# One-column products of a decode-attention backward pass, streamed 48 columns wide with a stride-0 operand

## The chip, the cores and the metric

One core of a Trainium2 chip. The metric is device time of one launch in microseconds (us). The kernel before takes 462.21 us (median of 3 runs, 458.82 to 466.44). A run can fall in a slow state (e1's profiled run took 472.17 us, its other three 458.97 to 465.29); all comparisons below use fast runs. A ratio is the mean time of one kernel's fast runs over that of the other's from the same rounds, so it isn't quite the ratio of the medians quoted beside it.

## The reference, cut to what matters

A gated mix of two branches, forward and backward in one launch. The branch that costs the time is attention of a single query over a cache: 32 heads, 4,096 keys of 128 values each, bf16.

```python
scores = einsum("bhqd,bhkd->bhqk", q, k_cache) * Dh ** -0.5   # one query per head
p = softmax(scores)
o = einsum("bhqk,bhkd->bhqd", p, v_cache)
out = g * (o @ wo) + (1 - g) * mlp(x)
# and the gradients of everything, among them dK and dV of all 32 heads
```

K and V are read (2.1 MB per head) and dK and dV written (2.1 MB per head); with the weights 165 MB cross the memory interface. Since there is one query, S = K q, dP = V dO, o = V'p and dq = K'ds are all matrix times vector.

## The kernel before

For S and dP the contraction runs over the head dimension, and the kernel transposes K and V for them. A head's K tile is `[128, 32, 128]` bf16; the kernel views two neighbouring bf16 as one fp32 and transposes 128x128 fp32 blocks on TensorE, 16 for K and 16 for V. ScalarE copies each four of them out of the PSUM tile that they were written to (256 copies of 587 ns on average). Then each product loads 128x128 weights and streams one or two columns; the page counts 5,916 weight loads to 5,916 matmuls.

```python
def transposes(src, c):                       # line L550: fp32 transposes; L552: the copy out
    ...
    nc.tensor.transpose(tp[:, t, :], flat[:, k * P:(k + 1) * P], ident_f[:])
    ...
    nc.scalar.copy(sb[...], tp[...])

def products(out, tb, c, vec):                # L559: S and dP, 2 columns each, 64 per head
    for t in range(4):
        k = c * 4 + t
        for par in range(2):
            nc.tensor.matmul(out[:, 2 * k:2 * k + 2], lhsT=tb[:, t, par, :], rhs=vec[:, par, :],
                             start=(par == 0), stop=(par == 1))

# in period(h), one head:
S, Z, O, MM = A[:, 0:J], A[:, 32:64], A[:, 64:65], A[:, 128:256]        # one PSUM tile
DP, DQ, PT = B[:, 0:J], B[:, 64:65], B[:, 128:256]                      # another
for j in range(J):                            # L618: o, 1 column, 32 per head
    nc.tensor.matmul(O, lhsT=vts[h][:, j, :], rhs=st["e"][:, j:j + 1], ...)
for j in range(J):                            # L670: dq, 1 column, 32 per head
    nc.tensor.matmul(DQ, lhsT=kts[h][:, j, :], rhs=ds[:, j, 0:1], ...)
```

VectorE multiplies the outer products dK and dV (L574). Loads are issued by SyncE in program order. K and V come three heads ahead, when the K buffer of the head before is released by its last dq product (SyncE waited 302.2 us for these products, in 27 waits); every fourth head the weights for a later group are loaded, behind that head's K and V:

```python
for h in range(H):
    hh, g = h % G, h // G                     # groups of G = 4 heads
    load_k(h + 3)
    load_v(h + 3)
    if hh == 0 and g + 1 < NG:
        prep_steps(g + 1, h)                  # q of the next group: needs wq; dO: needs wo
    if hh == 3:
        load_wo(g + 2)
        if g % 2 == 0:
            load_wq(g // 2 + 1)
    period(h)
```

Of the kernel before, what the change touches and what calls it, by code (L numbers as in the profile page):

```python
# [8 lines left out]
ALU = mybir.AluOpType  # L9
# [7 lines left out]
def kernel(  # L17
# [24 lines left out]
    nc = tc.nc  # L42
    P = 128
# [3 lines left out]
    J = Sk // P  # L47
    RC = D // P
    G = 4
    NG = H // G  # L50
    GD = G * Dh
    WG = 8
# [14 lines left out]
    dwq_v = out_4.rearrange("(rc r) c -> r rc c", r=P)  # L67
    wo_v = A_wo.rearrange("(g p i) n -> g p i n", p=P, i=G)
    dwo_v = out_5.rearrange("(g p i) n -> g p i n", p=P, i=G)
    w1_v = B_w1.rearrange("(rc r) f -> r rc f", r=P)  # L70
# [40 lines left out]
    kts, vts, wqs, wos = {}, {}, {}, {}  # L111
# [16 lines left out]
    def load_wo(g):  # L128
        if g < NG:
            wos[g] = wts.tile([P, G, D], BF16, name="wo_g", tag="wo_g", bufs=3)  # L130
            nc.sync.dma_start(wos[g][:], wo_v[g])
# [3 lines left out]
    def load_w2(c):  # L135
# [23 lines left out]
        out=ident_f[:], in_=ident_f[:], compare_op=ALU.not_equal, fill=1.0,  # L159
# [5 lines left out]
    nc.vector.tensor_copy(ident_bf[:], ident_f[:])  # L165
    mask4 = const.tile([P, 1, G], BF16, name="mask4")
    red4 = const.tile([P, P // G], BF16, name="red4")
# [62 lines left out]
    for i in range(3):  # L230
        t = const.tile([P, 2, G, 2, 2], BF16, name=f"qd2_{i}")
# [7 lines left out]
    def add(name, kind, fn, deps=(), head=0):  # L239
        steps.append((name, kind, fn, tuple(deps), head))  # L240
# [3 lines left out]
    def slot(h, p=2, d=1):  # L244

        slot_no[0] += 1
        room = {"P": p, "D": d, "T": 99}
        for kind in ("T", "D", "P"):
            for st in list(steps):
                name, k, fn, deps, head = st  # L250
                if k != kind or head > h or not room[k]:
                    continue
                if all(done.get(x, 1 << 30) < slot_no[0] for x in deps):
                    fn()
                    done[name] = slot_no[0]
                    steps.remove(st)
                    room[k] -= 1
# [70 lines left out]
    o_all = const.tile([P, H], BF16, name="o_all")  # L328
    dq_all = const.tile([P, H], BF16, name="dq_all")
# [213 lines left out]
    sts = {}  # L543

    def transposes(src, c):
        tp = tr_ps.tile([P, 4, P], F32, name="tr", tag="tr")
        flat = f32v(src[:].rearrange("p j d -> p (j d)"))
# [3 lines that stand above are left out]
        sb = tsb.tile([P, 4, P], F32, name="tT", tag="tT")  # L551
        nc.scalar.copy(sb[:].rearrange("p a b -> p (a b)"), tp[:].rearrange("p a b -> p (a b)"))  # L552
        return sb[:].rearrange("p a b -> p (a b)").bitcast(BF16).rearrange("p (a b two) -> p a two b", a=4, two=2)

    def products(out, tb, c, vec):
        for t in range(4):
            k = c * 4 + t
            for par in range(2):
                nc.tensor.matmul(out[:, 2 * k:2 * k + 2], lhsT=tb[:, t, par, :], rhs=vec[:, par, :],  # L559
                                 start=(par == 0), stop=(par == 1))  # L560

    def k_chunk(h, c, ts):
        ts.append(transposes(kts[h], c))

    def s_chunk(h, c, ts):
        gp = gps[h // G]
        if c == 0:
            sts[h] = {"A": sa_ps.tile([P, 512], F32, name="sA", tag="sA")}
        products(sts[h]["A"][:, 0:J], ts[c], c, gp["x2"][:, 0, h % G])

    def outer(dst, col, row, half):
        n = J // 2
# [7 lines left out]
    def dk_half(h, half):  # L580
        if h < 0:
            return
        st = sts[h]
        if half == 0:
            st["dK"] = outs.tile([P, J, Dh], BF16, name="dK_sb", tag="dVK")
        outer(st["dK"], st["ds"], gps[h // G]["qd"][:, 0, (h % G) * Dh:(h % G + 1) * Dh], half)
        if h == H - 1:
            a, b = half * (J // 2), (half + 1) * (J // 2)
            nc.gpsimd.dma_start(dKv[h][:, a:b, :], st["dK"][:, a:b, :])
        elif half == 1:  # L590
            nc.gpsimd.dma_start(dKv[h], st["dK"][:])  # L591
        if half == 1:
            sts.pop(h)
# [9 lines left out]
    def period(h):  # L603
        gp = gps[h // G]
        st = sts[h]
        nxt = h + 1 < H
        A = st["A"]
        S, Z, O, MM = A[:, 0:J], A[:, 32:64], A[:, 64:65], A[:, 128:256]
        B = st["B"] = sb_ps.tile([P, 512], F32, name="sB", tag="sB")
        DP, DQ, PT = B[:, 0:J], B[:, 64:65], B[:, 128:256]  # L610
        vec = gp["x2"][:, 1, h % G]
        tv, tk = [], []
        V = lambda c: tv.append(transposes(vts[h], c))
        dP = lambda c: products(DP, tv[c], c, vec)

        def o_part(a, b):
            for j in range(a, b):
                nc.tensor.matmul(O, lhsT=vts[h][:, j, :], rhs=st["e"][:, j:j + 1], start=(j == 0), stop=(j == J - 1))  # L618

        m32 = small.tile([P, 1], F32, name="m32", tag="m32")  # L620
        nc.vector.reduce_max(m32[:], S, axis=AX.X)  # L621
        V(0)
        dk_half(h - 1, 0)
        V(1)
        nc.tensor.transpose(MM, m32[:].to_broadcast([P, P]), ident_f[:])  # L625
        negM = small.tile([P, 1], F32, name="negM", tag="negM")
        nc.vector.tensor_reduce(negM[:], MM, axis=AX.X, op=ALU.max, negate=True)  # L627
        dk_half(h - 1, 1)
        e = st["e"] = small.tile([P, J], BF16, name="e_bf", tag="e_bf")
        V(2)  # L630
        dP(0)
        nc.scalar.activation(e[:], S, ACT.Exp, bias=negM[:], scale=1.0)
        V(3)
        dP(1)
        nc.tensor.matmul(Z, lhsT=ones_bf[:], rhs=e[:], start=True, stop=True)  # L635
        zs = small.tile([P, 1], F32, name="zs", tag="zs")
        nc.vector.reduce_sum(zs[:], Z, axis=AX.X)  # L637
        rz = st["rz"] = small.tile([P, 1], F32, name="rz", tag="rz")
        nc.vector.reciprocal(rz[:], zs[:])
        p_bf = st["p"] = small.tile([P, J, 2], BF16, name="p_bf", tag="p_bf")  # L640
        nc.scalar.activation(p_bf[:], e[:].unsqueeze(2).to_broadcast([P, J, 2]), ACT.Copy, scale=rz[:])
        dP(2)
        o_part(0, J)
        dP(3)
        slot(h)
        part = small.tile([P, 1], F32, name="part", tag="part")
        pj = small.tile([P, J], F32, name="pj", tag="pj", bufs=1)
        nc.vector.scalar_tensor_tensor(pj[:], in0=DP, scalar=1.0, in1=e[:], op0=ALU.mult, op1=ALU.mult,  # L648
                                       accum_out=part[:])
        dv_half(h, 0)  # L650
        nc.tensor.transpose(PT, part[:].to_broadcast([P, P]), ident_f[:])  # L651
        if nxt:
            k_chunk(h + 1, 0, tk)
            k_chunk(h + 1, 1, tk)
        dd = small.tile([P, 1], F32, name="dd", tag="dd")
        dj = small.tile([P, P], F32, name="dj", tag="dj", bufs=1)
        nc.vector.tensor_scalar(dj[:], PT, rz[:], None, ALU.mult, ALU.add, accum_out=dd[:])
        ds = st["ds"] = small.tile([P, J, 2], BF16, name="ds_bf", tag="ds_bf")
        nc.vector.scalar_tensor_tensor(ds[:], in0=DP.unsqueeze(2).to_broadcast([P, J, 2]), scalar=dd[:], in1=p_bf[:],  # L659
                                       op0=ALU.subtract, op1=ALU.mult)  # L660
        dv_half(h, 1)
        nc.vector.tensor_scalar(o_all[:, h:h + 1], O, rz[:], None, ALU.mult)
        if nxt:
            s_chunk(h + 1, 0, tk)
            k_chunk(h + 1, 2, tk)
        slot(h)
        if nxt:
            s_chunk(h + 1, 1, tk)
        for j in range(J):
            nc.tensor.matmul(DQ, lhsT=kts[h][:, j, :], rhs=ds[:, j, 0:1], start=(j == 0), stop=(j == J - 1))  # L670
        if nxt:
            k_chunk(h + 1, 3, tk)
            s_chunk(h + 1, 2, tk)
        nc.scalar.copy(dq_all[:, h:h + 1], DQ)  # L674
        if nxt:
            s_chunk(h + 1, 3, tk)
        kts.pop(h)
        vts.pop(h)
        slot(h)


    dwqt = {}
    CL = (NG - 1) * GD

# [19 lines left out]
    for h in range(H):  # L704
        hh, g = h % G, h // G
# [3 lines that stand above are left out]
            rest = steps[:]  # L709
# [10 lines left out]
        if h == H - 3:  # L720
            for rc in range(RC):
                add(f"dwq{rc}", "D", dwq_make(rc), (f"dqb{NG - 2}",), h + (rc + 1) // 2)
                add(f"dwqs{rc}", "T", lambda rc=rc: dwq_store(rc), (f"dwq{rc}",), h)
# [79 lines left out]
```

## Time and profile before

| | before |
|---|---|
| time | 462.21 us, profile 462.1 us |
| TensorE busy / mean granted clock | 84% / 0.61 |
| VectorE busy | 67% |
| DMA | 164.93 MB, 357 GB/s on average |
| fp32 transposes (L550) | 1,024 |
| one- and two-column products of S, dP, o and dq | 4,096 |

"Granted clock" is the share of full speed that the page gives for TensorE. In the row PEclk of the page each digit is one of 40 slices of the span, in tenths; 5 is half speed. The nines at its start are no full clock: the record of the clock begins near 20 us, and transposes at 15.35 us ran at the half-clock pace (eight in 1.78 us). The row DMA shows in tenths how busy the 16 DMA engines were. The lines themselves stand in the prediction.

### The profile page before, as it was taken

How to read it: one execution, taken by the hardware profiler on the slowest of the kernel's cores; microseconds unless marked ns; L12 is line 12 of the kernel's file. 1: busy time of each engine (PE TensorE's matmuls, PEld its weight loads, DVE VectorE, ACT ScalarE, POOL GpSimd, SP SyncE). 2: the span in 40 equal slices, each digit the busy share in tenths (PEclk: the TensorE clock that was granted, in tenths of full speed). 3: DMA queues.
4: the chain of work that ended last, by engine and by line, in shares of the span. 5: the costliest groups of instructions: out<-in, count | busy, mean ns of one | idle time of the engine just before them, and what ended most of it. 6: DMA issues, size and time to landing. Idle time of an engine off the chain costs nothing.

```text
span 462.1 us, 13671 instructions
## 1 busy us (share of the span) xinstructions
PE 389.3 (84%) x5916; PEld 363.1 (79%) x5916; DVE 311.1 (67%) x785; ACT 186.3 (40%) x410; POOL 49.3 (11%) x95
## 2 busy tenths in 40 slices
PE   2799999999999999799988999799898999999600
PEld 1688989899888888788877888788887888888500
DVE  4275443745578877787758876767768977777892
ACT  2444333443434444354443444345543544444200
POOL 0000000000000100010000110002100100011321
PEclk9965555656556665687565656656656756556555
DMA  7999999958798899999999899997999999845995
GB/s 268 416 382 372 424 419 418 359 242 319 309 374 313 321 386 381 419 399 331 419 422 364 308 399 393 409 411 280 374 396 357 380 395 377 338 179 218 400 405 200
DMA packets 26328, 164.93 MB, mean 357 GB/s; under 512 B 2812, under 2 KB 2812, under 8 KB 10012
## 3 DMA queue, kind: packets, MB, share of 16 engines
q1 hardware_dynamic: 14156, 82.03, 46.1%
q0 software_dynamic: 12112, 82.03, 44.3%
q8 instruction: 46, 0.75, 0.6%
q14 instruction: 14, 0.11, 0.1%
HBM read 82.03 MB, written 82.03 MB: 355 GB/s over the span
## 4 chain that ended last, share of the span: by engine, by line
PE 61%; DMA 18%; DVE 9%; ACT 7%; issue 2%; SPq 0%; ACTq 0%; DVEq 0%
PE tr L550 35%; DMA wo_g<-in_A_wo_dram 10%; DMA wq_g<-in_A_wq_dram 8%; ACT tT L552 5%; PE sB L670 5%; PE sA L559 5%; PE h_ps L404 3%; PE sA L618 3%; PE sB L559 2%; DVE junk L375 2%; DVE junk L278 2%; PE sB L651 2%; PE sA L625 1%; DVE zs L637 1%; PE ap_ps L356 1%
## 5 line engine op out<-in xcount | busy, mean ns | idle before, releaser
L552 ACT COPY tT<-tr 128x512 f32<-128x512 f32 x256 | 148.9, 587 | 206.2 <-PE tr L550 205.2
L550 PE MATMUL tr<-ident_f,Kn 128*128 128x128 f32 x512 | 121.8, 400 | 0.0
L550 PE MATMUL tr<-ident_f,Vn 128*128 128x128 f32 x512 | 119.9, 396 | 0.0
L559 PEld LDWEIGHTS <-tT 128*128 128x128 bf16 x2048 | 90.1, 107 | 36.6 <-ACT tT L552 29.5
L550 PEld LDWEIGHTS tr<-ident_f,Vn 128*128 128x128 f32 x512 | 93.3, 209 | 0.0
L550 PEld LDWEIGHTS tr<-ident_f,Kn 128*128 128x128 f32 x512 | 91.7, 207 | 0.3 <-issue 0.3
L574 DVE TENSOR_TENSOR dV_sb<-p_bf,qd 128x2048 bf16<-128x2048 bf16 x64 | 77.9, 1218 | 0.0
L574 DVE TENSOR_TENSOR dK_sb<-ds_bf,qd 128x2048 bf16<-128x2048 bf16 x64 | 77.7, 1216 | 0.0
L559 PE MATMUL sA<-qd,tT 128*128 128x2 bf16 x1024 | 48.4, 168 | 19.0 <-ACT dq_all L674 12.8
L559 PE MATMUL sB<-qd,tT 128*128 128x2 bf16 x1024 | 44.0, 166 | 0.0
L621 DVE TENSOR_REDUCE m<-sA 128x1 f32<-128x32 f32 x32 | 6.1, 192 | 51.9 <-PE sA L559 42.4
L601 POOL DMA_DIRECT2D out_dram<-dV_sb x32 | 17.6, 551 | 184.5 <-DVE dV_sb L574 127.8
L591 POOL DMA_DIRECT2D out_dram<-dK_sb x31 | 16.6, 535 | 190.8 <-DVE dK_sb L574 170.9
L618 PEld LDWEIGHTS <-Vn 128*128 128x128 bf16 x1024 | 31.2, 100 | 5.0 <-issue 5.0
L618 PE MATMUL sA<-e_bf,Vn 128*128 128x1 bf16 x1024 | 30.8, 164 | 3.0
L670 PE MATMUL sB<-ds_bf,Kn 128*128 128x1 bf16 x1024 | 31.6, 165 | 1.7 <-DVE ds_bf L659 1.2
L278 DVE SCALAR_TENSOR_TENSOR junk<-wo_g,da_bc 128x640 bf16<-128x640 bf16 x32 | 26.3, 822 | 8.6 <-DMA wo_g<-in_A_wo_dram 8.0
L670 PEld LDWEIGHTS <-Kn 128*128 128x128 bf16 x1024 | 29.7, 103 | 2.0 <-issue 2.0
L627 DVE TENSOR_REDUCE negM<-sA 128x1 f32<-128x128 f32 x32 | 9.3, 291 | 25.6 <-PE sA L625 25.6
L375 DVE SCALAR_TENSOR_TENSOR junk<-wq_g,dq_bc 128x1024 bf16<-128x1024 bf16 x20 | 24.3, 1216 | 0.1
L637 DVE TENSOR_REDUCE zs<-sA 128x1 f32<-128x32 f32 x32 | 6.1, 192 | 21.9 <-PE sA L635 21.6
L651 PE MATMUL sB<-ident_f,part 128*128 128x128 f32 x32 | 13.2, 413 | 8.7 <-DVE pj L648 8.5
(144 smaller groups left out, 313.9 us busy)
## 6 DMA issues: line engine op xcount, KB each, us to landing
Kn<-in_A_k_cache_dram SPq DMA_DIRECT2D x32, 1024.0 KB, 7.8
Vn<-in_A_v_cache_dram SPq DMA_DIRECT2D x32, 1024.0 KB, 13.9
out_dram<-dV_sb POOLq DMA_DIRECT2D x32, 1024.0 KB, 6.5
out_dram<-dK_sb POOLq DMA_DIRECT2D x31, 1024.0 KB, 8.7
wq_g<-in_A_wq_dram SPq DMA_DIRECT2D x4, 1280.0 KB, 6.4
wo_g<-in_A_wo_dram SPq DMA_DIRECT2D x8, 640.0 KB, 14.3
out_dram<-wo_g POOLq DMA_DIRECT2D x8, 640.0 KB, 9.7
out_dram<-dwq_t POOLq DMA_DIRECT2D x5, 896.0 KB, 8.8
```

The lines of the kernel that those rows point to most:

```text
L278: nc.vector.scalar_tensor_tensor(junk[:, 0:D], in0=wos[g][:, i, :], scalar=1.0, in1=da_bc[:], op0=ALU.mult, op1=ALU.mult, accum_out=gp["do ...
L375: nc.vector.scalar_tensor_tensor(junk[:], in0=wqs[w][:, rc, :], scalar=1.0, in1=dq_bc[:, w * WG * Dh:(w + 1) * WG * Dh], op0=ALU.mult, op1 ...
L404: nc.tensor.matmul(hps["t"][:, fc:fc + 1], lhsT=w1_sb[:, rc, :].rearrange("p (q c) -> p q c", c=FCN)[:, :, fc], rhs=x_bf[:, rc:rc + 1], st ...
L550: nc.tensor.transpose(tp[:, t, :], flat[:, k * P:(k + 1) * P], ident_f[:])
L552: nc.scalar.copy(sb[:].rearrange("p a b -> p (a b)"), tp[:].rearrange("p a b -> p (a b)"))
L559: nc.tensor.matmul(out[:, 2 * k:2 * k + 2], lhsT=tb[:, t, par, :], rhs=vec[:, par, :], start=(par == 0), stop=(par == 1))
L574: nc.vector.tensor_tensor(dst[:, a:b, :].rearrange("p j (a b) -> p j a b", b=2), col[:, a:b, :].unsqueeze(2).to_broadcast([P, n, Dh // 2, 2]),
L591: nc.gpsimd.dma_start(dKv[h], st["dK"][:])
L601: nc.gpsimd.dma_start(dVv[h], st["dV"][:])
L618: nc.tensor.matmul(O, lhsT=vts[h][:, j, :], rhs=st["e"][:, j:j + 1], start=(j == 0), stop=(j == J - 1))
L651: nc.tensor.transpose(PT, part[:].to_broadcast([P, P]), ident_f[:])
L670: nc.tensor.matmul(DQ, lhsT=kts[h][:, j, :], rhs=ds[:, j, 0:1], start=(j == 0), stop=(j == J - 1))
```

## The change

The intent is to keep TensorE's clock up by streaming more columns. A product that needs one column (S and dP: two) now streams 48 that all read the same column, through an operand with stride 0. The wanted result is in the first columns of the output. The others fall on columns that a later product starts afresh, or on free columns of the tile, so Z, o, dq and the transposed maxima move further back.

```diff
+    W = 48
 def products(out, tb, c, vec):
-                nc.tensor.matmul(out[:, 2 * k:2 * k + 2], lhsT=tb[:, t, par, :], rhs=vec[:, par, :],
+                nc.tensor.matmul(out[:, 2 * k:2 * k + W], lhsT=tb[:, t, par, :],
+                                 rhs=vec[:, par, :].unsqueeze(1).to_broadcast([P, W // 2, 2]),
                                  start=(par == 0), stop=(par == 1))
...
-        S, Z, O, MM = A[:, 0:J], A[:, 32:64], A[:, 64:65], A[:, 128:256]
+        S, Z, O, MM = A[:, 0:J], A[:, 96:96 + J], A[:, 128:128 + W], A[:, 256:384]
-        DP, DQ, PT = B[:, 0:J], B[:, 64:65], B[:, 128:256]
+        DP, DQ, PT = B[:, 0:J + W], B[:, 128:128 + W], B[:, 256:384]
...
-                nc.tensor.matmul(O, lhsT=vts[h][:, j, :], rhs=st["e"][:, j:j + 1], ...)
+                nc.tensor.matmul(O, lhsT=vts[h][:, j, :], rhs=st["e"][:, j:j + 1].to_broadcast([P, W]), ...)
...
-            nc.tensor.matmul(DQ, lhsT=kts[h][:, j, :], rhs=ds[:, j, 0:1], ...)
+            nc.tensor.matmul(DQ, lhsT=kts[h][:, j, :], rhs=ds[:, j, 0:1].to_broadcast([P, W]), ...)
```

(Cut: readers of DP, O and DQ take their first columns. Line numbers of the changed kernel are one to four higher: L550 becomes L551, L559 L560, L618 L620, L670 L673.)

More of the change, by code (lines that the diff above doesn't have):

```diff
@@ L568, in s_chunk @@
             sts[h] = {"A": sa_ps.tile([P, 512], F32, name="sA", tag="sA")}
-        products(sts[h]["A"][:, 0:J], ts[c], c, gp["x2"][:, 0, h % G])
+        products(sts[h]["A"][:, 0:J + W], ts[c], c, gp["x2"][:, 0, h % G])
     def outer(dst, col, row, half):
@@ L617, in o_part @@
             for j in range(a, b):
-                nc.tensor.matmul(O, lhsT=vts[h][:, j, :], rhs=st["e"][:, j:j + 1], start=(j == 0), stop=(j == J - 1))
+                nc.tensor.matmul(O, lhsT=vts[h][:, j, :], rhs=st["e"][:, j:j + 1].to_broadcast([P, W]),
+                                 start=(j == 0), stop=(j == J - 1))
         m32 = small.tile([P, 1], F32, name="m32", tag="m32")
@@ L647, in period @@
         pj = small.tile([P, J], F32, name="pj", tag="pj", bufs=1)
-        nc.vector.scalar_tensor_tensor(pj[:], in0=DP, scalar=1.0, in1=e[:], op0=ALU.mult, op1=ALU.mult,
+        nc.vector.scalar_tensor_tensor(pj[:], in0=DP[:, 0:J], scalar=1.0, in1=e[:], op0=ALU.mult, op1=ALU.mult,
                                        accum_out=part[:])
@@ L658, in period @@
         ds = st["ds"] = small.tile([P, J, 2], BF16, name="ds_bf", tag="ds_bf")
-        nc.vector.scalar_tensor_tensor(ds[:], in0=DP.unsqueeze(2).to_broadcast([P, J, 2]), scalar=dd[:], in1=p_bf[:],
+        nc.vector.scalar_tensor_tensor(ds[:], in0=DP[:, 0:J].unsqueeze(2).to_broadcast([P, J, 2]), scalar=dd[:], in1=p_bf[:],
                                        op0=ALU.subtract, op1=ALU.mult)
         dv_half(h, 1)
-        nc.vector.tensor_scalar(o_all[:, h:h + 1], O, rz[:], None, ALU.mult)
+        nc.vector.tensor_scalar(o_all[:, h:h + 1], O[:, 0:1], rz[:], None, ALU.mult)
         if nxt:
@@ L669, in period @@
         for j in range(J):
-            nc.tensor.matmul(DQ, lhsT=kts[h][:, j, :], rhs=ds[:, j, 0:1], start=(j == 0), stop=(j == J - 1))
+            nc.tensor.matmul(DQ, lhsT=kts[h][:, j, :], rhs=ds[:, j, 0:1].to_broadcast([P, W]),
+                             start=(j == 0), stop=(j == J - 1))
         if nxt:
@@ L673, in period @@
             s_chunk(h + 1, 2, tk)
-        nc.scalar.copy(dq_all[:, h:h + 1], DQ)
+        nc.scalar.copy(dq_all[:, h:h + 1], DQ[:, 0:1])
         if nxt:
```

## The prediction

> **What bounds the kernel now.** I read the page first, for the shares, the clock and the last chain.
>
> ```profile
> PEclk9965555656556665687565656656656756556555
> DMA  7999999958798899999999899997999999845995
> ...
> PE 61%; DMA 18%; DVE 9%; ACT 7%; issue 2%; SPq 0%; ACTq 0%; DVEq 0%
> PE tr L550 35%; DMA wo_g<-in_A_wo_dram 10%; DMA wq_g<-in_A_wq_dram 8%; ACT tT L552 5%; PE sB L670 5%; PE sA L559 5%; PE h_ps L404 3%; PE sA L618 3%; PE sB L559 2%; DVE junk L375 2%; DVE junk L278 2%; PE sB L651 2%; PE sA L625 1%; DVE zs L637 1%; PE ap_ps L356 1%
> ```
>
> TensorE carries 61% of the chain that ended last, more than half of that in its fp32 transposes (L550). Its granted clock sits near half speed (mean 0.61 in the record). The DMA row is almost as full: nines nearly everywhere. So there are two limits, close together, and the question is how much lies between them.
>
> Second, the timeline of TensorE, once at half clock and once at full clock (start, length):
>
> ```profile
> 31.94 1.91 PE L550 MATMUL tr<-ident_f,Vn 128*128 128x128 f32 x8
> 33.65 0.42 PE L625 MATMUL sA<-ident_f,m 128*128 128x128 f32 x1
> ...
> 36.59 0.99 PE L618 MATMUL sA<-e_bf,Vn 128*128 128x1 bf16 x32
> 37.45 0.35 PE L559 MATMUL sB<-qd,tT 128*128 128x2 bf16 x8
> ```
> ```profile
> 356.75 1.04 PE L550 MATMUL tr<-ident_f,Vn 128*128 128x128 f32 x8
> 357.63 0.27 PE L625 MATMUL sA<-ident_f,m 128*128 128x128 f32 x1
> ...
> 359.72 0.94 PE L618 MATMUL sA<-e_bf,Vn 128*128 128x1 bf16 x32
> 360.52 0.34 PE L559 MATMUL sB<-qd,tT 128*128 128x2 bf16 x8
> ```
>
> From start to next start, eight transposes take 1.71 us at half clock and 0.88 us at full clock: 214 against 110 ns each. Thirty-two one-column products take 0.86 and 0.80 us: 27 against 25 ns. So the clock is worth 104 ns on a transpose and almost nothing on a one-column product.
>
> Third, stretches of 3.41 us, transposes alone (PE busy with count, weight loads, clock, DMA share, GB/s):
>
> ```profile
> 415.67:419.08 3.41, 3.23 (x13) 2.69 (x14) 0.50 0.61 243
> 419.08:422.49 3.41, 1.22 (x11) 1.07 (x11) 1.00 0.55 226
> 422.49:425.91 3.42, 2.23 (x10) 1.48 (x9) 0.50 0.30 117
> ```
>
> A stretch dense in transposes (13, 3.23 us of 3.41) is followed by one at full clock; that one, with 11 transposes and one-column products between them, is followed by half clock. I counted columns for the whole trace: 256 cycles for an fp32 transpose [...], its column count for any other matmul, on a grid of 3.413 us whose offset I fitted to 0.1 us. All 24 stretches followed by full clock hold 3,120 cycles or more; all 111 followed by half clock hold fewer. One threshold[...] serves stretches at either clock. Adding weight per instruction for small products makes the separation worse: they count by their columns, hence almost for nothing.
>
> [...] The trace shows 25 and 27 ns at one column; no wide bf16 product with its own weight load runs between 2 and 128 columns in numbers[...].
>
> **The change part by part.** Instruction order and waits are the same on all five engines in the built programs; only the width of four kinds of product changes (32 each of S, dP, o and dq per head, 128 in all, 4,096 in the kernel). Offsets inside the two PSUM banks move[...].
>
> - [...]
> - What it does to the clock: a head now streams 34 fp32 transposes x 256 = 8,700 cycles and some 200 for the rest. The change adds nearly 128 x 48 = 6,140: about 15,000. At before's 12.5 us per head that was 8,900 x 3.41 / 12.5 = 2,430 per window, under the threshold; now, even at 14.2 us per head, 3,600, above it; at 10 us, 5,100. So TensorE should get the full clock in nearly all windows where it isn't waiting.
> - Worth on TensorE: 34 x 104 ns = 3.5 us per cold head. A head without extra work, at half clock throughout, takes 12.5 us; it would take about 9.0. Before already spends about a quarter of the heads' time warm (clock 0.60 to 0.67 in the middle), so some 2.8 us on average: 32 x 2.8 = 90 us of TensorE time.
>
> Most of those 90 us can't reach the end. The stretches of heads 0-3, 4-7 and so on (cut at the reduction that opens a head), with the columns PE, weight loads, DVE, ACT, POOL, clock, DMA share, GB/s:
>
> ```profile
> 20.67:77.00 56.33, 52.74 (x731) 50.12 (x731) 26.66 (x69) 22.17 (x49) 3.86 (x7) 0.55 1.02 403
> 77.00:135.33 58.33, 55.08 (x789) 52.02 (x789) 34.15 (x97) 22.95 (x52) 4.79 (x9) 0.59 0.83 325
> 135.33:184.39 49.06, 45.56 (x714) 42.42 (x714) 38.82 (x93) 22.79 (x50) 4.79 (x9) 0.60 0.91 350
> 184.39:235.09 50.70, 44.64 (x744) 41.82 (x744) 37.61 (x97) 22.38 (x50) 5.38 (x10) 0.67 1.01 395
> 235.09:288.39 53.30, 46.95 (x744) 43.96 (x744) 39.04 (x95) 22.83 (x50) 5.30 (x10) 0.60 0.95 373
> 288.39:341.66 53.27, 47.59 (x732) 44.59 (x732) 37.84 (x96) 24.50 (x52) 6.31 (x11) 0.60 0.96 370
> 341.66:390.68 49.02, 44.01 (x714) 41.05 (x714) 39.18 (x92) 22.44 (x50) 4.78 (x9) 0.64 0.97 385
> 390.68:427.52 36.84, 34.59 (x518) 32.11 (x518) 27.01 (x62) 16.25 (x34) 4.88 (x8) 0.55 0.62 250
> 427.52:462.10 34.58, 9.24 (x145) 7.82 (x144) 23.72 (x55) 3.67 (x9) 8.27 (x11) 0.50 0.84 334
> ```
>
> For each group I take the largest of length x DMA share, PE length less the clock's gain, and DVE with some waits:
> heads 0-3: DMA full, 55.5 (saves 1);
> 4-7: DMA 48.4, PE 58.3 - 11 = 47, so 49.5 (saves 9);
> 8-11: DMA 44.6, DVE 38.8 plus waits, so 46 (saves 3);
> 12-15: 50 (saves 1);
> 16-19: 51 (saves 2.5);
> 20-23: 51 (saves 2);
> 24-27: 48 (saves 1);
> 28-30: reads are over, DMA 0.62, PE 9.3 and DVE 9.0 per head plus waits, 3 x 9.6 = 29 (saves 8);
> last stretch: DVE and stores, PE only 9.2 of 34.6 us, saves 1.
> Sum 28 us: 462 - 28 = 434. I add 2 us because no group reaches its floor exactly: **436 us**.
>
> **The rivals.**
> - The clock does not rise, because a stride-0 operand isn't counted[...]. Against it: the count is by columns, whatever matmul they belong to (four 128-column bf16 ones made the difference in some windows). No moving operand with stride 0 runs in before.
> - The clock rises, but DMA takes it all. For it: shares of 0.95 and more in five groups, and weights (wo_g, wq_g) already in the chain for 10% and 8%. A faster TensorE asks for them earlier, and they stand behind K and V of three heads ahead. Only heads 4-11 and 28-30 gain: about 445 to 452 us.
> - DMA gives more than its share suggests: before moves 164.93 MB at 357 GB/s on average, 424 in its best slices; 164.93 MB / 0.424 = 389 us, plus some 25 us of start and end: 414 us. Against it: the rate at full share varies from 330 to 425 even now.
> - DVE becomes the bound, 9.0 to 9.8 us per head of the middle groups: close to TensorE's 9.0, but below DMA's 11 to 12.7. It costs something only inside a group.
>
> **Range and chances.** The middle is the sum, 436. The lower end, 422, is the third rival half true; the upper end, 451, the second rival in full. Faster by over 2% means under 453 us: 0.84. Within 2%: 0.12 (DMA or weight waits eat it). Slower: 0.04 (the clock stays down[...]).
>
> **What would show each step.** Clock: the row PEclk at 0.8 or more in most slices, mean over 0.8 against 0.61; transposes 110 ns apart. Products: 32 of them still in 0.80 to 0.86 us[...]. Heads inside a group 9.5 to 10.5 us, the first head of a group from the fourth on 16 to 20 us, waiting for wq_g or wo_g: the gain handed to DMA. The chain: PE's 61% falls under 45%, DMA's 18% at least doubles. DMA share 0.95 or more from 20 us until the last read. The prediction is wrong if the clock stays near 0.6, [...] or if groups 12-27 get much shorter than 48 us each, which would say that DMA share wasn't a floor.

## The result, and the profile after

440.36 us (median of 4 runs, 438.39 to 443.84) against 462.86 us of before in the same rounds; ratio 0.955, 95% interval 0.945 to 0.965. The result is correct. The profiled run took 436.6 us from first to last instruction.

The same rows of the page, now of the changed kernel:

```profile
PEclk9999686696899999589995999859997899999655
DMA  7999999986899999989999899999999999998994
...
DMA 33%; DVE 32%; PE 18%; issue 9%; ACT 4%; SPq 1%; POOL 1%; ACTq 0%; POOLq 0%
```

The clock is full in most slices, its mean 0.873 instead of 0.61. TensorE's share of the chain that ended last fell from 61% to 18%; DMA has the largest share, with VectorE close behind it.

TensorE's timeline of the changed kernel, once at full clock and once at half (start, length, with the next instruction's start below):

```profile
169.08 1.07 PE L551 MATMUL tr<-ident_f,Vn 128*128 128x128 f32 x8
169.99 0.27 PE L628 MATMUL sA<-ident_f,m 128*128 128x128 f32 x1
...
172.09 0.96 PE L620 MATMUL sA<-e_bf,Vn 128*128 128x48 bf16 x32
172.89 0.36 PE L560 MATMUL sB<-qd,tT 128*128 128x48 bf16 x8
```
```profile
50.78 1.46 PE L673 MATMUL sB<-ds_bf,Kn 128*128 128x48 bf16 x32
52.06 0.87 PE L551 MATMUL tr<-ident_f,Kn 128*128 128x128 f32 x4
```

Thirty-two products of 48 columns take 0.80 us at full clock, 25 ns each: exactly what one column took. At half clock they take 1.28 us, 40 ns each. Eight transposes take 0.91 us, 114 ns each, where before took 214 at half clock.

The same stretches as in the prediction, cut at the reduction that opens a head (columns: length, then busy time and count of PE, weight loads, DVE, ACT, POOL, then clock, DMA share, GB/s; the last stretch is left out, it is in the table below):

```profile
20.34:71.07 50.73, 45.79 (x731) 42.88 (x730) 26.40 (x70) 21.24 (x49) 3.87 (x7) 0.85 1.02 413
71.07:130.41 59.34, 49.08 (x790) 45.64 (x790) 34.23 (x98) 22.24 (x52) 4.81 (x9) 0.84 0.88 339
130.41:169.28 38.87, 33.80 (x715) 30.97 (x714) 37.86 (x94) 21.41 (x50) 4.81 (x9) 1.00 1.01 404
169.28:221.56 52.28, 36.36 (x745) 33.37 (x744) 37.15 (x97) 21.41 (x50) 5.38 (x10) 0.87 0.98 380
221.56:272.96 51.40, 35.67 (x745) 32.98 (x744) 38.33 (x96) 21.49 (x50) 5.32 (x10) 0.90 0.97 386
272.96:326.38 53.42, 36.66 (x733) 33.91 (x732) 37.35 (x95) 23.18 (x52) 6.33 (x11) 0.87 0.97 379
326.38:373.10 46.72, 35.74 (x715) 32.90 (x714) 38.35 (x91) 21.41 (x50) 4.96 (x9) 0.89 1.00 397
373.10:401.00 27.90, 24.68 (x519) 22.58 (x518) 26.35 (x64) 15.10 (x34) 5.23 (x8) 1.00 0.94 391
...
```

| heads | before | predicted | measured |
|---|---|---|---|
| 0-3 | 56.3 | 55.5 | 50.7 |
| 4-7 | 58.3 | 49.5 | 59.3 |
| 8-11 | 49.1 | 46 | 38.9 |
| 12-15 | 50.7 | 50 | 52.3 |
| 16-19 | 53.3 | 51 | 51.4 |
| 20-23 | 53.3 | 51 | 53.4 |
| 24-27 | 49.0 | 48 | 46.7 |
| 28-30 | 36.8 | 29 | 27.9 |
| 31 and end | 34.6 | 33.6 | 35.6 |

TensorE's busy time fell by 75 us, from 389.3 to 313.9, but the span by 25.5. In heads 12 to 27, half of all heads, 206.3 us became 203.8. There the gain was taken back in one place, the first head of each group. Two heads of the changed kernel show it, the last of one group and the first of the next (same columns):

```profile
160.11:169.28 9.17, 7.97 (x165) 7.31 (x164) 8.54 (x23) 4.91 (x11) 1.07 (x2) 1.00 1.01 424
169.28:192.07 22.79, 10.88 (x199) 9.98 (x198) 10.66 (x29) 5.82 (x14) 1.07 (x2) 0.70 0.98 391
```

Inside a group a head takes 9.2 us where a cold one took 12.5; the first head takes 22.8, and TensorE is busy for half of it. The list of waits of the changed kernel says for what (total us, times, longest):

```profile
DVE junk L279 <- DMA wo_g<-in_A_wo_dram: 33.3, 6, 10.7
...
PE qc_ps L269 <- DMA wq_g<-in_A_wq_dram: 28.9, 4, 11.9
```

Both are weights for the next group. In before these waits were 8.0 and 5.7 us. SyncE's queue shows when they were asked for:

```profile
162.45 0.33 SPq L132 DMA_DIRECT2D wo_g<-in_A_wo_dram  x1
162.87 0.88 SPq L127 DMA_DIRECT2D wq_g<-in_A_wq_dram  x1
167.68 0.33 SPq L117 DMA_DIRECT2D Kn<-in_A_k_cache_dram  x1
...
190.48 0.33 SPq L117 DMA_DIRECT2D Kn<-in_A_k_cache_dram  x1
```

They are issued at 162.45 us and needed some 10 us later, in head 12, but stand behind the K and V of head 14, issued from 158.51 us. While TensorE waits it releases no K buffer, so no further load of K is issued from 167.68 to 190.48 us.

**The clock count again.** The clock record of before holds only 0.50 and 1.00, and its periods, but for the one that the trace's end cuts off, are whole multiples of 3.413 us; 18 of its 21 periods at full clock last 3.413 us. The prediction's count (full clock after a stretch of 3.413 us with enough streamed cycles) was repeated for this document in the 13 packed traces. A cycle is one counted column; an fp32 transpose counts 256, since at half clock its 128 columns took 214 ns, 1.67 ns each, and the 48 of a wide product 40 ns, 0.83 ns each. The stretches were cut at one offset for all, with a product split where a stretch ends and half clock assumed before the record begins. Of 1,660 stretches, the 915 that are followed by full clock all hold at least 3,060 cycles, and the 745 followed by half clock at most 3,132; 14 lie between. In the changed kernel alone the two classes lie far apart: at least 3,301 in 90 stretches, at most 2,921 in 37. So in these traces the classes part near 3,100, known to some 2%; the single boundary just under 3,120 that the prediction found in before is sharper than the counting allows. A further weight for each product, whatever its width, sorts worse: with 16 cycles each, the best threshold puts 76 of the 1,660 on the wrong side, with none 5.

### The profile page after: what moved, and what is told of

Same layout as the page of the kernel before. It is cut to its first block, busy times and chain, and to the rows that moved or that the text cites. A ratio compares the mean times of both kernels' runs of the same rounds, so it can differ in the third digit from the quotient of the medians.

```text
span 436.6 us, 13671 instructions
## 1 busy us (share of the span) xinstructions
PE 313.9 (72%) x5916; PEld 288.1 (66%) x5916; DVE 306.5 (70%) x785; ACT 177.2 (41%) x410; POOL 50.7 (12%) x95
## 4 chain that ended last, share of the span: by engine, by line
DMA 33%; DVE 32%; PE 18%; issue 9%; ACT 4%; SPq 1%; POOL 1%; ACTq 0%; POOLq 0%
DMA wq_g<-in_A_wq_dram 11%; DMA wo_g<-in_A_wo_dram 9%; DVE dK_sb L576 8%; DVE dV_sb L576 7%; DMA Kn<-in_A_k_cache_dram 6%; PE tr L551 6%; DVE junk L376 5%; DMA Vn<-in_A_v_cache_dram 4%; ACT tT L553 3%; DMA out_dram<-wo_g 3%; PE sB L673 2%; PE sA L560 2%; PE sA L620 2%; PE h_ps L405 2%; DVE junk L506 1%
## 5 line engine op out<-in xcount | busy, mean ns | idle before, releaser
L553 ACT COPY tT<-tr 128x512 f32<-128x512 f32 x256 | 142.8, 589 | 158.1 <-PE tr L551 156.9
L560 PEld LDWEIGHTS <-tT 128*128 128x128 bf16 x2048 | 80.6, 98 | 40.8 <-ACT tT L553 34.9
L551 PE MATMUL tr<-ident_f,Kn 128*128 128x128 f32 x512 | 84.9, 305 | 0.9 <-DMA Kn<-in_A_k_cache_dram 0.9
L551 PE MATMUL tr<-ident_f,Vn 128*128 128x128 f32 x512 | 75.1, 284 | 0.0
L560 PE MATMUL sA<-qd,tT 128*128 128x48 bf16 x1024 | 49.7, 189 | 23.6 <-ACT dq_all L678 12.5
L551 PEld LDWEIGHTS tr<-ident_f,Kn 128*128 128x128 f32 x512 | 64.3, 157 | 1.5 <-PE sB L654 1.2
L551 PEld LDWEIGHTS tr<-ident_f,Vn 128*128 128x128 f32 x512 | 58.9, 146 | 0.0
L279 DVE SCALAR_TENSOR_TENSOR junk<-wo_g,da_bc 128x640 bf16<-128x640 bf16 x32 | 26.3, 822 | 33.9 <-DMA wo_g<-in_A_wo_dram 33.3
L560 PE MATMUL sB<-qd,tT 128*128 128x48 bf16 x1024 | 46.1, 183 | 0.0
L673 PE MATMUL sB<-ds_bf,Kn 128*128 128x48 bf16 x1024 | 34.0, 189 | 2.2 <-DVE ds_bf L662 1.4
L620 PEld LDWEIGHTS <-Vn 128*128 128x128 bf16 x1024 | 30.2, 96 | 7.5 <-issue 7.5
L620 PE MATMUL sA<-e_bf,Vn 128*128 128x48 bf16 x1024 | 30.7, 183 | 4.7 <-DVE zs L640 2.7
L673 PEld LDWEIGHTS <-Kn 128*128 128x128 bf16 x1024 | 31.2, 100 | 2.6 <-issue 2.6
L269 PE MATMUL qc_ps<-cols_bf,wq_g 128*128 128x1 bf16 x160 | 5.3, 165 | 28.9 <-DMA wq_g<-in_A_wq_dram 28.9
## 6 DMA issues: line engine op xcount, KB each, us to landing
out_dram<-dK_sb POOLq DMA_DIRECT2D x31, 1024.0 KB, 10.7
```

Of the source, the lines that this page charges most:

```text
L269: nc.tensor.matmul(qc_ps[:, hh:hh + 1], lhsT=wq[:, rc, off + hh * Dh:off + (hh + 1) * Dh], rhs=x_bf[:, rc:rc + 1], start=(rc == 0), stop=( ...
L279: nc.vector.scalar_tensor_tensor(junk[:, 0:D], in0=wos[g][:, i, :], scalar=1.0, in1=da_bc[:], op0=ALU.mult, op1=ALU.mult, accum_out=gp["do ...
L553: nc.scalar.copy(sb[:].rearrange("p a b -> p (a b)"), tp[:].rearrange("p a b -> p (a b)"))
L560: nc.tensor.matmul(out[:, 2 * k:2 * k + W], lhsT=tb[:, t, par, :], rhs=vec[:, par, :].unsqueeze(1).to_broadcast([P, W // 2, 2]), start=(pa ...
```

## The experiments

Theory after the result: the gain is the clock; the clock is earned by streamed columns, whatever streams them; the rest of the clock's worth is lost to DMA. Rivals: the new places in PSUM help by themselves; the widening of particular products matters; what is left is not DMA's throughput but the order in which its queue serves loads, or TensorE itself. Eleven kernels were run. All times of before below are medians of the runs that belong to the same call. The calls of the experiments ran on three different chips; before's medians there, 462.52, 462.56 and 463.04 us, agree with the 462.86 us above, so times of different calls are set side by side below.

### e1_layout: the new places, narrow products

```diff
-  matmul(out[:, 2 * k:2 * k + W], ..., rhs=vec[:, par, :].unsqueeze(1).to_broadcast([P, W // 2, 2]))
+  matmul(out[:, 2 * k:2 * k + 2], ..., rhs=vec[:, par, :])          # likewise o and dq: 1 column
```

> The changed kernel with its new PSUM offsets, but the four kinds of product narrow again (2 and 1 columns). Theory (the gain is the clock, earned by streamed columns): nothing is earned, so 460 to 466 us, ratio to before 0.99 to 1.01, granted clock 0.59 to 0.63. Rival (the new places of S, Z, o and dq in their banks help by themselves): below 455 us with the clock still near 0.61.

463.12 us against 462.52 of before; ratio of fast runs 0.999 (0.991 to 1.007). One of its four runs, the profiled one, was in the slow state (472.17 us) and isn't used. The places in PSUM do nothing that is seen within 1%. This rival falls.

### e2_w16: a third of the width

```diff
-    W = 48
+    W = 16
```

> The changed kernel at a width of 16 columns: 128 x 16 = 2,048 cycles are added per head to before's 8,900. Theory: in a cold 12.5 us head that makes a mean of 2,990 cycles per 3.41 us window, just under the threshold of about 3,120, so densest windows reach it more often; once warm, a head of 9.5 us brings 3,930 per window and the clock stays. So most of the gain: granted clock 0.78 to 0.87, 440 to 449 us. Rival (width must be near what TensorE can stream in an issue slot, so gain goes with width): a third of the gain, clock near 0.70, 455 us.

446.32 us against 462.52, ratio 0.966 (0.961 to 0.970); clock 0.773. A third of the width gives three quarters of the gain (1 - 0.966 against 1 - 0.955), as a threshold does and a proportional effect does not. The clock came out just under the range. In the recount its stretches part at the same place: at most 3,046 cycles before half clock, at least 3,062 before full clock.

### e3_w96: twice the width

```diff
-    W = 48
+    W = 96
     # Z, o and dq moved to columns 128 and 160 to make room
```

> Width 96: [...] Theory (DMA bounds the changed kernel, TensorE has slack in most of it): clock at 0.87 or more, heads inside a group 11 to 11.5 us instead of 9.2, the first heads of the middle groups shorter by as much as the other three grow; only heads 4 to 7 and 28 to 31 lose: 445 to 456 us. Rival (TensorE is still what bounds it): 490 to 510 us.

455.44 us against 462.52, ratio 0.986 (0.981 to 0.991); clock 0.936. In its timeline 32 dq products at full clock take 1.40 us from their start (300.51) to the next transposes' (301.91), 44 ns each where 48 columns took 25, so TensorE got some 2.4 us more work per head (128 x 19 ns). What a product of 96 columns costs was the author's estimate before this run. The stretches of heads 8-11, 12-27 and 28-30:

```profile
134.59:179.79 45.20, 42.14 (x715) 39.86 (x714) 38.68 (x93) 21.67 (x50) 4.79 (x9) 1.00 0.96 372
179.79:385.08 205.29, 175.57 (x2932) 165.91 (x2931) 152.78 (x379) 88.74 (x202) 21.95 (x40) 0.96 0.97 382
385.08:418.43 33.35, 31.12 (x519) 29.25 (x518) 26.66 (x63) 15.37 (x34) 5.43 (x8) 1.00 0.73 289
```

In heads 12 to 27 TensorE is busy 31 us longer than in the changed kernel (175.57 against 36.36 + 35.67 + 36.66 + 35.74 = 144.43), and the stretch lasts 205.3 us instead of 203.8. TensorE had that slack, and it lay where the expectation put it: the four first heads of these groups took 68 us together instead of 87, the other twelve 137 instead of 117. In heads 8-11 and 28-30 a head grew on average from 9.7 to 11.3 us and from 9.3 to 11.1, and those stretches grew by 6.3 and 5.5 us: there the head itself is the bound. That heads 8-11 would lose I had not expected.

### e4_odq96: only o and dq wide, the same number of columns

```diff
-    W = 48
+    W = 96
     # products() narrow as in before: 2 columns
```

> Only o and dq wide, at 96 columns, S and dP narrow: 64 x 96 columns, the same 6,140 per head as in the changed kernel. Theory (columns count, whichever product streams them): clock 0.82 to 0.89 and 438 to 446 us, although half of the products are as before[...]. Rival (it matters that S and dP, on the path to the softmax, run wide or without gaps): clock under 0.75 and over 450 us.

456.03 us against 462.52, ratio 0.986 (0.980 to 0.992); clock 0.886. Half right. The clock is where the column count puts it (changed kernel: 0.873), although S and dP are narrow, so here it made no difference to the clock which product streams the columns. The time is 10 us over the expected range. Heads inside a group take 10.3 to 10.7 us, 1.2 us more each; the expected range left next to no room for that, but in heads 8-11 and 28-30 it is not hidden (42.4 and 31.3 us against 38.9 and 27.9). Heads 12-27 took 208.6 us, 4.8 more than in the changed kernel. Why this kernel isn't faster than e3, with half of its extra work, is not settled; one of its four runs, 462.68 us, was in the slow state and isn't in the ratio.

### e5_halfdv_after and e6_halfdv_before: a tenth of the traffic less

```diff
-            nc.gpsimd.dma_start(dVv[h], st["dV"][:])
+            nc.gpsimd.dma_start(dVv[h][:, 0:J // 2, :], st["dV"][:, 0:J // 2, :])
```

Half of dV is not written, so both results are wrong on purpose; the other outputs are right.

> The changed kernel storing only the first half of each head's dV (half of dV stays unwritten, so the result is wrong on purpose): 0.52 MB less per head, 16.8 MB of 165. Nothing else changes. Theory (DMA sets the pace of heads 8 to 27): at some 0.4 MB per us the saved traffic is 42 us of DMA, of which groups of heads 12 to 27 keep 4 to 6 us each until DVE and TensorE (37 to 40 us a group) bound them, heads 0 to 3 about 2: 412 to 424 us. Rival (the waits for weights are latency in the queue, or the compute chain bounds): 435 us or more.

> The same cut in the kernel before (result wrong on purpose). Theory (there TensorE at half clock bounds most heads at 12 to 12.5 us, DMA only the first head of each group): 448 to 460 us, a gain of 3% at most and less than half of what the same cut gives the changed kernel. Rival (both kernels were bound by DMA to the same degree): the same saving as in the changed kernel, 15 us or more more.

The cut takes the changed kernel to 415.93 us (ratio to before 0.902, 0.896 to 0.908): 24.4 us less than 440.36. It takes before to 456.56 us (ratio 0.988, 0.980 to 0.997): 6.0 us less than 462.56. Heads 12 to 27 of the two, e5 and then e6:

```profile
162.67:352.09 189.42, 143.41 (x2932) 132.18 (x2931) 151.13 (x378) 87.42 (x202) 21.92 (x40) 0.92 0.95 370
```
```profile
185.84:387.28 201.44, 186.29 (x2931) 174.51 (x2931) 153.72 (x380) 92.86 (x202) 21.71 (x40) 0.59 0.92 346
```

14.4 of the 24.4 us come from these heads in the changed kernel (203.8 to 189.4); in before 4.9 (206.3 to 201.4). So with the clock up these heads wait for traffic far more than with the clock down, although both kernels took nearly the same time for them. What the run does not show is that the total of bytes is the limit. The whole gain lies in the four first heads of the groups (72.5 us together instead of 87.2; the other twelve heads took 116.9 and 116.7), and the waits for wq and wo fell from 28.9 and 33.3 us to 17.4 and 20.4. Fewer bytes under way while the weights come would do the same. In before the four first heads gained too, 8.1 us (62.5 to 54.4), and the other twelve lost 3.3 at a lower clock (0.59, before 0.62). The next run keeps all bytes and changes only their order.

### e7_weights_early: the order of the queue

A first version gave the weights more buffers and loaded them two heads earlier; it did not build (this attempt is not in the record). The run changes the order alone:

```diff
-        load_k(h + 3)
-        load_v(h + 3)
+        if hh != 3:
+            load_k(h + 3)
+            load_v(h + 3)
...
         if hh == 3:
             load_wo(g + 2)
             if g % 2 == 0:
                 load_wq(g // 2 + 1)
+            load_k(h + 3)
+            load_v(h + 3)
```

> The changed kernel with the loads of wo and wq put ahead of, not behind, the K and V loads issued in the same head; correct result. In the changed kernel TensorE waits 28.9 us for wq and DVE 33.3 us for wo. Theory (DMA is full 98% of the time from head 8 to head 30, so a wait taken away here comes back as another): 432 to 442 us, first heads of groups shorter, another head of the group longer. Rival (these waits are the order of the queue and cost their full length): 415 to 425 us.

423.76 us against 462.56 of before, ratio 0.920 (0.914 to 0.926): 16.6 us less than the changed kernel with not a byte less. My theory fell here; the rival's range holds. The waits and heads 12 to 27 of e7:

```profile
PE qc_ps L269 <- DMA wq_g<-in_A_wq_dram: 22.2, 4, 11.2
DVE junk L279 <- DMA wo_g<-in_A_wo_dram: 9.3, 3, 3.6
```
```profile
164.41:349.77 185.36, 143.05 (x2932) 131.78 (x2931) 150.81 (x378) 87.35 (x202) 21.93 (x40) 0.92 1.01 411
```

The wait for wo fell from 33.3 to 9.3 us, and the 16 heads took 185.4 us instead of 203.8. The last two columns show how that can be: the share went from 0.97-1.00 to 1.01, which is little, but at that share 411 GB/s crossed instead of about 385. By the page's queue shares the 16 engines were busy 95.4% of 436.6 us in the changed kernel, 417 us, and 97.0% of 420.5 us in e7, 408 us; idle 20 and 13 us. So a share near 1 was not a floor: the same bytes went through in less busy time. The slow stretches come after a stall, not in it: from 176 to 184 us, while TensorE waits for wq, the changed kernel moves 412 GB/s at a share of 1.03, but from 204 to 212 us only 300 GB/s at 0.96. The packed trace shows which packets stretch: from 204 to 212 us a load's packet of 8 KB took 457 ns on average and a store's 323, where from 141 to 169 us both took 313 to 314. Why the loads' packets take longer there is not settled by these runs.

### e11_before_early: the same order without the clock

The edit of e7 on the kernel before.

> The kernel before (narrow products) with the loads of wo and wq ahead of K and V. Theory: with TensorE at half clock it waits only 5.7 us for wq, and DVE 8.0 us for wo, so the order is worth a third of what it is worth to the changed kernel at most: 454 to 461 us. Rival (the order of the queue was a bound of its own, clock or not): 445 to 450 us.

453.86 us against 463.04, ratio 0.980 (0.973 to 0.987): 9.2 us. The order helps at half clock too, more than the third I allowed at most, though less than the 16.6 us that it gives at full clock. The time is just under the expected range. So the order costs something in both kernels, and it seems to cost more at the higher clock.

### e8_wide_h: the products that still streamed one column

The first layer of the MLP has 90 one-column products in heads 2 to 6. They come about 180 ns apart at either clock (15 in 2.68 us at half clock in before, 15 in 2.69 us in the changed kernel, most of them at full clock), so while they run almost no columns are streamed.

```diff
-                    nc.tensor.matmul(hps["t"][:, fc:fc + 1], ..., rhs=x_bf[:, rc:rc + 1], ...)
+                    nc.tensor.matmul(hps["t"][:, fc:fc + 128], ..., rhs=x_bf[:, rc:rc + 1].to_broadcast([P, 128]), ...)
```

> The changed kernel with the products of the MLP's first layer, which still stream one column each 179 ns, made 128 columns wide [...]. They are in heads 2 to 6, where the changed kernel's clock falls to half for a third to a half of the time. Theory (columns earn the clock): the clock stays full through heads 2, 3, 5 and 6; heads 5 and 6, which DMA does not fill (shares 0.69 and 0.89), lose 1 to 2.5 us each: 434 to 439 us. Rival (the wide products run slower than 179 ns each): 90 of them, slower by 30 ns or more, 442 us or more.

437.94 us against 462.56, ratio 0.950 (0.945 to 0.955): 2.4 us less than the changed kernel, with overlapping intervals, so a small gain at best. Clock 0.891. Fifteen of the wide products, at full clock, took 2.75 us, 183 ns each: nearly free, as expected. Head 6 ran at full clock throughout and took 12.8 us instead of 14.5; heads 2 and 3 together 27.3 instead of 31.5. But head 4 grew from 18.0 to 21.3 us, waiting for wq: most of it was given back at the next wait.

### e9_both and e10_prep_late: a version that beats both

e9 joins e7 and e8. e10 also starts the preparation of the next group one head later, so that it asks for wq later:

```diff
-        if hh == 0 and g + 1 < NG:
+        if hh == 1 and g + 1 < NG:
```

> Weights ahead of K and V, and the first-layer products of the MLP 128 wide: the two edits that gave 424 and 438 us, together; correct result. Revised theory (the changed kernel is bound by DMA only through the order of its queue: in order, weights needed first stood behind K and V needed later): the gains of 16 and 2 us are in different heads and add up to 420 to 423 us. Rival (DMA is now the floor, full from end to end): 424 us, no gain from the second edit.

> As the run with both edits, and the preparation of the next group of heads starts one head later, so that its first product asks for wq some 9 us later; it is done a head before it is needed; correct result. With weights ahead of K and V TensorE still waits 22 us for wq in three places. Theory of the queue's order: most of those waits go, 412 to 419 us. Rival (DMA is the floor: 165 MB at the best rate seen, 424 bytes per ns, is 389 us, and packets took 408 us of 16 engines' time in the profile of weights ahead): 419 to 424 us, the wait comes back at K or V.

Both are correct. e9: 422.66 us, ratio 0.916 (0.912 to 0.921); 1.1 us better than e7. That is inside the expected range, but the intervals of the two ratios overlap, so it isn't shown that the second edit adds anything here. e10: 420.33 us against 463.04, ratio 0.912 (0.908 to 0.916). The wait for wq shrank only to 17.9 us and 11.5 us of waits for K came up; the rival's range holds. Its two rows of the page:

```profile
PEclk9999999999999999769898899968999999998555
DMA  7999999999999999999999999999999999999950
```

DMA is full from the second slice to the last but two. 164.92 MB in 416.5 us are 396 GB/s. e10 is the best of all correct versions, 42.7 us under before. Less traffic, not more TensorE, looks like the next step; no run tried it on this version.

## Why the prediction was right or wrong

The prediction was 436 us, 422 to 451; measured 440.36. The steps one by one:

1. **The clock follows streamed columns, with one threshold.** Right. The same threshold fits the changed kernel (at least 3,301 cycles before full clock, at most 2,921 before half); nothing is earned by layout alone (e1), three quarters of the gain at a third of the width (e2), and as much clock by wide o and dq alone (e4).
2. **48 columns cost nothing at full clock.** Right: 25 ns measured, as one column took; at half clock they took 40. What 48 columns would cost was the author's estimate: the trace of before shows 25 and 27 ns for one column, and hardly a wider product with weights of its own. At 96 columns a product took 44 ns at full clock (e3).
3. **About 90 us of TensorE's time go.** Measured 75: the clock's mean is 0.87, not 1, because TensorE now waits long enough for it to fall at the start of groups, and because of step 6.
4. **Only some 28 us of it reach the end.** Right in size: 25.5 us in the profiles, 22.5 in the medians. The group heads paid it back in waits for wq and wo, as the second rival said; they took 18 to 24 us, more than the 16 to 20 predicted, and heads inside groups mostly 9.2 to 10.6. DMA's share of the chain went from 18 to 33%, a little less than the doubling I asked for.
5. **Length times DMA share is a floor for each group.** This step failed, though its sum came out. First, a group is not a unit: K and V come three heads ahead and stores can lag, so bytes move between groups. Heads 8-11 took 38.9 us, under their floor of 44.6, and moved fewer bytes (404 GB/s x 38.87 us = 15.7 MB; before 350 x 49.06 = 17.2 MB). Heads 0-3, with a share of 1.02 in both kernels, took 50.7 us instead of 56.3 and moved 21.0 MB instead of 22.7. The bytes of heads 8-11 did not come in the next four groups (heads 12 to 27 moved 78.5 MB, before 78.4) but at the end: heads 28 to 30 moved 10.9 MB instead of 9.2. Second, a share near 1 did not mean that no more could cross: e7 moved the same bytes 16.6 us faster (411 GB/s at 1.01 in heads 12 to 27, about 385 at 0.97 to 1.00 in the changed kernel). The sign named for this failure, groups 12-27 much shorter than 48 us, did not show in the changed kernel (46.7 to 53.4 us), and yet the floor was false. Nor was the rule kept to: for heads 0-3 and 12-15 length times share is 57.5 and 51.2 us, more than their lengths, and 55.5 and 50 were set by eye. The third rival of the prediction, that DMA gives more than its share suggests, named 414 us; e10 reached 420.
6. **Heads 4-7 gain 9 us.** Wrong: they lost 1. I subtracted the clock's gain from TensorE's time and forgot what I had listed for later groups: head 4 needs wq as well, and TensorE waited 5.1 us for it (from 76.1 to 81.2 us). And the MLP's narrow products let the clock fall in this group (0.84; 0.89 in e8, where they are wide). So TensorE's busy time fell by 6.0 us (55.1 to 49.1) instead of 11, and its idle time grew by 7.0. DMA's share in this group was 0.88, under the 0.95 that the prediction asked for until the last read.
7. **Heads 28-30, where reads are over, are set by TensorE and VectorE.** Right: 27.9 us against 29 predicted and 36.8 before. e3 and e4, which lengthen exactly these heads, confirm it.

The sum fits in part by luck. The errors of the nine stretches add up to 31 us without their signs and cancel to under 3 (heads 8-11 7 us and heads 0-3 5 us better than predicted, heads 4-7 10 us worse). What was right by its mechanism is the clock and its cost, and that waits for weights take most of the gain back.

## What to carry to other kernels

Count the columns that TensorE streams, not its busy time: with one- and two-column products it was busy for 84% of the span at a mean clock of 0.61; with 48 columns, 25 ns each at full clock like one, the mean was 0.873. When a faster engine only meets a wait elsewhere, look at the order of the loads in the queue before believing that memory is full; a kernel with a DMA share of 0.98 over half of its heads still had 16 us in its queue's order. And test a bound by taking traffic or work away on both sides of the change, as with half of dV: it tells two kernels of equal time apart. It does not tell throughput from order; for that, keep the bytes and change the order, as e7 did.

## What the traces show beyond the prediction

- The fp32 transposes of `nc.tensor.transpose` count towards the clock: in before a 3.41 us stretch at half clock with 13 of them (3.23 us busy, 415.67 to 419.08 us) was followed by full clock, and so were all its stretches with at least 3,120 counted cycles, most of them from transposes.
- Streamed columns told the stretches apart, busy time did not: of two stretches of before at half clock, each with TensorE busy for 3.14 us, the one with 8 transposes (313.27 to 316.68 us) was followed by half clock, the next, with 12, by full clock. In the 13 traces the two classes, told apart at about 3,100 cycles at either clock, overlap only between 3,060 and 3,132; the number of products, each with its weight load, sorts worse.
- With weights taken 18 elements apart in memory, products of the MLP's first layer came about 180 ns apart: 179 ns with one column at half clock, 183 with 128 columns at full clock. That the distance in memory is the cause is not shown: no run takes these weights without it.
- DMA at nearly the same busy share moved 385 GB/s or 411 GB/s in the same 16 heads, depending on the order of loads (0.97 to 1.00 in the changed kernel, 1.01 in e7).
